# Loading one pair of heads through a second DMA queue and shifting matmuls in an attention + GeGLU kernel

## The chip, the cores and the metric

The kernel runs on one core of a Trainium2 chip. The metric is the device time of one execution in microseconds (us), as the median of several runs. Most executions of one kernel agree within 0.3%. Ratios are the mean time of one kernel's runs over the mean time of the other's in the same rounds, so they are not quite the ratio of the medians quoted beside them. The kernels were measured on different chips. Kernels are compared only within the same rounds.

Names used below: PE is TensorE (matmuls), PEld its weight loads, DVE is VectorE, ACT is ScalarE, POOL is GpSimd, SP is SyncE. "The landing" of a load is the time at which all 16 DMA engines have reported their part.

## The reference

Attention over 8 batches and 8 heads with 16 beacon keys ahead of 576 causal keys, then a GeGLU block over all 4608 tokens.

```python
B, H, S, Nb, D = (8, 8, 576, 16, 64)
k_all = np.concatenate([beacon_k, k], axis=2)          # v_all likewise
scores = scale * np.matmul(q, k_all.transpose(0, 1, 3, 2))
scores = np.where(causal, -1000000000.0, scores)       # only over the 576 keys
a = softmax(scores);  attn = np.matmul(a, v_all)
x = attn.transpose(0, 2, 1, 3).reshape(B * S, H * D)   # 4608 x 512
out = (gelu(x @ w_gate) * (x @ w_val)) @ w_out         # d_ff = 1536
```

## The kernel before

Everything is computed in bf16 with fp32 accumulation. Batch 0 is the start: nothing is on the chip yet, so q and k come in pairs of heads ("pair 0" is heads 0-1, and so on). GpSimd's queue loads them with a cast from fp32 to bf16, TensorE transposes them, and the evictions of those transposes make the operands of the scores.

```python
    load_qk6(0, 0, 2)                # k, then q of heads 0-1, on GpSimd's queue
    load_qk6(0, 2, 4, (1,))          # k of heads 2-3
    # ... GpSimd builds the identity `eye` here
    load_qk6(0, 2, 4, (0,))          # q of heads 2-3
    load_qk6(0, 4, 6)
    load_qk6(0, 6, H)
    # ... then v, the weights, batch 1
```

```python
    warm(66)                         # 66 small matmuls while the loads are under way
    # ... casts of the beacons and the mask, on VectorE
    transpose_both(0, 0)             # pair 0: 12 + 13 transposes, two evictions
    c((0, 0))                        # scores of pair 0, column chunk 0, then ScalarE's exponential
    c((0, 2))
    transpose_both(0, 1)             # pair 1: needs k and q of heads 2-3
    c((0, 1))
    c((1, 0))
    # ... pairs 2 and 3
    c((3, 0))
    c((3, 2))
    av_head(0, 0, 0, psum_t, "t")    # exponentials times v
    av_head(0, 0, 1, psum_o, "o")
    c((2, 3), (3, 3))
    # ... then the first gate/value matmuls of the GeGLU block
```

In batches 1 to 7 the scores and values of batch b are interleaved with the out matmuls of batch b-1; `o(n)` emits the next n of 48. Scores go into three PSUM buffers, and each buffer is free again when ScalarE has taken its exponential.

```python
            o(4)
            scores(b, (0, 0)); scores(b, (0, 2)); scores(b, (0, 1))   # one call per line in the file
            o(5)
            # ...
            o(4)
            scores(b, (0, 3), (1, 3)); scores(b, (1, 0)); scores(b, (1, 2))
            # ...
            o(6)
            av_head(b, 0, 0, psum_t, "t")
            o(1)
            scores(b, (1, 1)); scores(b, (2, 0)); scores(b, (2, 2))
            # ...
            av_head(b, 0, 1, psum_t, "t")
            o(6)
            scores(b, (2, 1)); scores(b, (2, 3), (3, 3)); scores(b, (3, 0))
```

The softmax here doesn't subtract the row's maximum and nothing guards it: scores larger than these inputs give would overflow.

Of the kernel before, what the change touches and what calls it, by code (L numbers as in the profile page):

```python
# [7 lines left out]
P = 128  # L8
B, H, S, NB, D = 8, 8, 576, 16, 64
SK = S + NB  # L10
N_TOK = B * S
D_MODEL = 512
# [28 lines left out]
FP32 = mybir.dt.float32  # L41
# [8 lines left out]
def kernel(  # L50
# [12 lines left out]
    nc = tc.nc  # L63
    keep = tc.keep_in_program_order
# [8 lines left out]
    opool = ctx.enter_context(tc.tile_pool(name="opool", bufs=2))  # L73
# [17 lines left out]
    NRING = 2  # L91
    q_ring, k_ring, v_ring = [], [], []
# [11 lines left out]
    qkT_by_tile = qkT_sb.rearrange("p (w j m c) -> p w j m c", w=2, j=5, m=NPAIR)  # L104
    nc.vector.memset(qkT[:, :, 1, SK:640], 0.0)
    nc.vector.memset(qkT[:, :, 0, 0:NB], 0.0)

    for r in range(NRING):
        nc.vector.memset(q_ring[r][0:32, 0, :, :], 0.0)
        nc.vector.memset(q_ring[r][64:P, 4, :, :], 0.0)  # L110
        nc.vector.memset(k_ring[r][64:P, 4, :, :], 0.0)

    neg = const.tile([P, 256], BF16, name="neg", tag="neg")

    def dma(out_ap, in_ap):
        keep(nc.gpsimd.dma_start(out=out_ap, in_=in_ap))  # L116

    qk6 = {}

    def qk6_of(b):  # L120
        if b not in qk6:
            qk6[b] = (
                hpool.tile([P, 2, H, 6 * D], BF16, name="qk6", tag="hT_sb"),
                kpool.tile([NB, H, D], BF16, name="kb", tag="kb"),
            )
        return qk6[b]

    def load_qk6(b, h0, h1, ws=(1, 0)):
        for w in ws:
            src = (q, k)[w]  # L130
            dma(
                qk6_of(b)[0][0:96, w, h0:h1, :],
                src[b, h0:h1, :, :].rearrange("h (p r) d -> p h (r d)", r=6),
            )
# [18 lines left out]
    def load_qk(b):  # L153
        for load in qk_loads(b):
            load()
# [51 lines left out]
    def transpose_half(b, m, w, by_act=False):  # L207
        pool, tag = ((psum_o, "o"), (psum_t, "t"))[w]
        t_ps = pool.tile([P, 1024], BF16, name="t_ps", tag=tag)
        for _ in range(8 if by_act else 0):  # L210
            tr(t_ps[0:D, 640:768], idle[:, 0:D])
        tr_part(b, m, w, t_ps)
        out_ap = qkT[:, m, w, NB:SK].rearrange("p (t r) -> p t r", r=6)
        in_ap = t_ps[:, 0:S].rearrange("p (r t) -> p t r", r=6)
        if by_act:
            act(out_ap, in_ap, ACT.Copy)
        else:
            keep(nc.vector.tensor_copy(out_ap, in_ap))  # L218
        return t_ps

    def beacon_part(m, t_ps):
        keep(nc.vector.tensor_copy(qkT[:, m, 1, 0:NB], t_ps[:, S:SK]))  # L222

    def transpose_both(b, m):
        k_ps = transpose_half(b, m, 1)
        transpose_half(b, m, 0, by_act=m == 0)
        beacon_part(m, k_ps)
# [86 lines left out]
    def attend(b, m, hi, x_ps):  # L314
        expT, v_sb = exp_ring[:, m, :, :], v_ring[b % NRING]
        for j in range(5):
            for t in range(j + 1):
                e0 = EXP_OFF[t] + (j - t) * P
                mm(
                    x_ps[:, j * DV : (j + 1) * DV],  # L320
                    expT[0 : KROWS[t], hi, e0 : e0 + P],
                    v_sb[0 : KROWS[t], t, 2 * m + hi, 0:DV],
                    t == 0,
                    t == j,
                    skip_group_check=True,
                )
# [26 lines left out]
    def av_head(b, m, hi, pool, tag):  # L353
        x = pool.tile([P, 1, 512], FP32, name="x_ps", tag=tag)
        attend(b, m, hi, x[:, 0, :])
        normalize(b, m, x, hi, hi + 1)
# [39 lines left out]
    def gv_mms(ci, fi, *kks, split=False, last=False):  # L396
        if (ci, fi) not in gv_of:
            if split:
                gv_of[ci, fi] = (
                    psum_t.tile([P, CH], FP32, name="g_ps", tag="t"),  # L400
                    psum_s.tile([P, 2, CH], FP32, name="v_ps", tag="s")[:, 0, :],
                )
            else:
                gv_ps = psum_s.tile([P, 2, CH], FP32, name="gv_ps", tag="s")
                gv_of[ci, fi] = (gv_ps[:, 0, :], gv_ps[:, 1, :])
        n0 = ci * CH

        def part(w):
            for kk in kks:
                mm(  # L410
                    gv_of[ci, fi][w],
                    (wg_sb, wv_sb)[w][:, kk, fi * P : (fi + 1) * P],
                    xT_sb[:, kk, n0 : n0 + CH],
                    kk == 0,
                    last and kk == kks[-1],
                    skip_group_check=True,
                )

        part(0)
        if not split:  # L420
            part(1)
        if not last:
            return
        ge_sb = fpool.tile([P, CH], BF16, name="ge_sb", tag="ge_sb")
        act(ge_sb, gv_of[ci, fi][0], ACT.Gelu)
        if split:
            part(1)
        if ci not in h_of:
            h_of[ci] = hpool.tile([P, F_TILES, CH], BF16, name="hT_sb", tag="hT_sb")
        keep(  # L430
            nc.vector.tensor_tensor(  # L431
                out=h_of[ci][:, fi, :], in0=gv_of.pop((ci, fi))[1], in1=ge_sb, op=ALU.mult
            )
        )
# [30 lines left out]
    def out_mms(ci, u0, u1):  # L465
        for u in range(u0, u1):
# [11 lines left out]
    kb_sb = opool.tile([NB, H, D], FP32, name="kb_sb", tag="o_sb")  # L478
    keep(nc.sync.dma_start(out=kb_sb, in_=beacon_k[0].rearrange("h t d -> t h d")))
    vb_sb = opool.tile([NB, H, D], FP32, name="vb_sb", tag="o_sb")  # L480
    keep(nc.sync.dma_start(out=vb_sb, in_=beacon_v[0].rearrange("h t d -> t h d")))
    load_qk6(0, 0, 2)
    load_qk6(0, 2, 4, (1,))
    keep(
        nc.gpsimd.affine_select(  # L485
            out=eye,
            in_=eye,
# [5 lines left out]
        )  # L493
    )
    load_qk6(0, 2, 4, (0,))
    load_qk6(0, 4, 6)
    load_qk6(0, 6, H)
    for load in key_loads(v, beacon_v, v_ring[0][:, :, :, 0:D], 0)[1:]:
        load()
# [12 lines left out]
    def ahead(n):  # L512
        for load in loads[:n]:
            load()
        del loads[:n]

    ahead(5)

    def c(*parts):
        scores(0, *parts)  # L520

    keep(nc.scalar.preload_act_table_set(SET_EXP))
    warm(66)
    keep(nc.vector.tensor_copy(qk6[0][1], kb_sb))
    keep(nc.vector.tensor_copy(v_ring[0][0:NB, 0, :, 0:D], vb_sb))
    keep(nc.vector.tensor_tensor_scan(neg, eye, idle, -1.0, ALU.add, ALU.add))
    keep(nc.vector.tensor_scalar_mul(neg, neg, -MASKED))
    transpose_both(0, 0)
    c((0, 0))
    c((0, 2))  # L530
    transpose_both(0, 1)
    c((0, 1))
    c((1, 0))
    c((1, 2))
    transpose_both(0, 2)
# [4 lines left out]
    c((2, 2))  # L540
    c((2, 1))
    c((3, 0))
    c((3, 2))
    av_head(0, 0, 0, psum_t, "t")
    av_head(0, 0, 1, psum_o, "o")
    c((2, 3), (3, 3))
    av(0, 1)
    c((3, 1))
# [13 lines left out]
    for kk in (1, 2, 3):  # L562
        for fi in (0, 1):
            gv_mms(0, fi, kk, last=kk == 3)
    for b in range(B):
        u = [0]

        def o(n):
            out_mms(b - 1, u[0], u[0] + n)
            u[0] += n  # L570

        if b:
            keep(nc.scalar.preload_act_table_set(SET_EXP))
            o(4)
            scores(b, (0, 0))
            scores(b, (0, 2))
            scores(b, (0, 1))
            o(5)
            if b == 1:
                transpose_pe(1, 3)  # L580
            ahead(2)
            o(4)
            scores(b, (0, 3), (1, 3))
            scores(b, (1, 0))
            scores(b, (1, 2))
            ahead(2)
            o(6)
            av_head(b, 0, 0, psum_t, "t")
            o(1)
            scores(b, (1, 1))  # L590
            scores(b, (2, 0))
            scores(b, (2, 2))
            ahead(2)
            av_head(b, 0, 1, psum_t, "t")
            turn_dma(b, 0)
            o(6)
            scores(b, (2, 1))
            scores(b, (2, 3), (3, 3))
            scores(b, (3, 0))
            av_head(b, 1, 0, psum_o, "o")  # L600
            o(5)
            av_head(b, 1, 1, psum_o, "o")
            turn_dma(b, 1)
            scores(b, (3, 1))
            scores(b, (3, 2))
            av(b, 2)
            turn_dma(b, 2)
            o(6)
            av(b, 3)
            turn_dma(b, 3)  # L610
            o(11)
            keep(nc.scalar.preload_act_table_set(SET_GELU))  # L612
            for kk in range(K_CHUNKS):
                for fi in range(2):
                    gv_mms(b, fi, kk, last=kk == 3)
        for fi in range(F_TILES):
            if fi >= 2:
                gate_val(b, fi, fi == F_TILES - 1 and b < B - 1)
            if b == 0 and fi in (6, 7, 9):
                transpose_pe(1, min(fi - 6, 2), by_act=True)  # L620
            if fi == 0:
                if b and b + 1 < B:
                    hold(b, 3)
                    load_v(b + 1)
                if b and b + 2 < B:
                    load_qk(b + 2)
                if 2 <= b + 1 < B:
                    transpose_dma(b + 1)
                store(nc.sync)
# [40 lines left out]
```

## Time and profile before

| | before |
|---|---|
| time, median of 3 runs | 367.49 us (367.24 to 367.71) |
| span of the profiled run | 366.2 us |
| PE busy | 355.5 us, 97% |
| first gate/value matmul of the GeGLU block | 22.45 us |
| distance between first scores of neighbouring batches | 39.16 us |

The page of the profile gives busy time per engine first, and then the span in 40 slices, where a digit is the busy share (or the granted TensorE clock) in tenths.

```profile
PE 355.5 (97%) x3127; PEld 183.6 (50%) x3170; DVE 154.8 (42%) x305; ACT 188.8 (52%) x243; POOL 161.7 (44%) x288
...
PE   6899999999999999999999999999999999999996
...
PEclk9999999999999999999999999999999999999999
```

PE is busy nearly everywhere, except in the first slices. So only the start has time to win, besides small stops in the loop. In the start, the chain that ended last (start in us, length in us, what) goes through one load:

```profile
3.83 5.19 DMA qk<-in_q_dram
9.03 0.04 issue
9.07 0.47 PE t_ps L181 x12
9.53 0.02 issue
9.56 0.76 DVE qkT L218
10.31 0.08 DVE qkT L222
10.40 0.05 issue
10.45 0.76 PE s_ps L173 x12
```

The load is q of heads 2-3. It was issued at 3.83 and landed at 9.03, and everything of pair 1 follows it. ScalarE's exponentials of this stage (start, length, group, count, idle time before it and what ended that):

```profile
10.03 9.59 ACT L176 ACTIVATE expT<-s_ps 128x992 bf16<-128x992 f32 x11 [0.68 <-PE s_ps L173]
```

ScalarE runs eleven exponentials without a gap once the scores come, so from 10 to 20 us it sets the pace.

### The profile page before, as it was taken

To read this page: it belongs to the slowest core of one execution; us is meant where nothing else is said; L and a number is where in the kernel's file an instruction comes from. 1 tells how busy PE (TensorE), PEld (TensorE's weight loads), DVE (VectorE), ACT (ScalarE), POOL (GpSimd) and SP (SyncE) were. 2 spreads that over 40 slices of the span, in tenths; PEclk is the share of its full clock that TensorE was granted. 3 is DMA by queue.
4 is the path that set the end of the run, shared out by engine and by line. 5 is a ranking of instruction groups with operands and counts; after the bars stand their busy time and mean duration, and the time that the engine had idled before them with its cause. 6 is when DMAs were issued, how large, how long until landed. Compare 5 with 4: busy or idle time off the path is not lost.

```text
span 366.2 us, 7625 instructions
## 1 busy us (share of the span) xinstructions
PE 355.5 (97%) x3127; PEld 183.6 (50%) x3170; DVE 154.8 (42%) x305; ACT 188.8 (52%) x243; POOL 161.7 (44%) x288
## 2 busy tenths in 40 slices
PE   6899999999999999999999999999999999999996
PEld 6664446444654456444644464445544564444443
DVE  6544545333454335343533354434444353333332
ACT  3973488237933594339723892369334953321210
POOL 8934387565537552845476454656230530000000
PEclk9999999999999999999999999999999999999999
DMA  7999999899069965999299927992795033000103
GB/s 102 172 203 204 197 124 91 135 197 163 20 124 141 213 52 65 163 209 77 56 144 211 122 38 117 170 198 29 100 155 125 11 66 116 0 0 30 57 31 114
DMA packets 160419, 41.57 MB, mean 114 GB/s; under 512 B 146944, under 2 KB 155904, under 8 KB 160384
## 3 DMA queue, kind: packets, MB, share of 16 engines
q0 software_dynamic: 104848, 19.11, 68.9%
q1 hardware_dynamic: 55536, 21.96, 29.7%
q8 instruction: 25, 0.41, 0.5%
q14 instruction: 10, 0.08, 0.1%
HBM read 38.27 MB, written 9.44 MB: 130 GB/s over the span
## 4 chain that ended last, share of the span: by engine, by line
PE 94%; DVE 2%; DMA 1%; issue 1%; POOL 1%; POOLq 0%
PE gv_ps L173 47%; PE o_ps L173 25%; PE x_ps L173 9%; PE s_ps L173 8%; PE v_ps L173 2%; PE g_ps L173 2%; DMA qk<-in_q_dram 1%; PE t_ps L181 1%; DVE qkT L218 1%; POOL qk L116 0%; PE y_ps L181 0%; DVE qkT L200 0%; DVE qkT L204 0%; POOL eye L485 0%; DVE o_sb L450 0%
## 5 line engine op out<-in xcount | busy, mean ns | idle before, releaser
L176 ACT ACTIVATE ge_sb<-gv_ps 128x512 bf16<-128x512 f32 x101 | 59.4, 597 | 142.6 <-PE gv_ps L173 141.5
L431 DVE TENSOR_TENSOR hT_sb<-gv_ps,ge_sb 128x512 bf16<-128x512 f32 x101 | 69.1, 691 | 115.4 <-ACT ge_sb L176 115.4
L173 PE MATMUL gv_ps<-xT_sb,wg_sb 128*128 128x512 bf16 x402 | 111.4, 379 | 0.5
L173 PE MATMUL gv_ps<-xT_sb,wv_sb 128*128 128x512 bf16 x388 | 107.9, 379 | 0.4
L176 ACT ACTIVATE expT<-s_ps 128x992 bf16<-128x992 f32 (+3 forms) x112 | 100.5, 973 | 8.7 <-PE s_ps L173 8.5
L173 PE MATMUL o_ps<-wo_sb,hT_sb 128*128 128x512 bf16 (+2 forms) x420 | 100.6, 373 | 2.1 <-issue 1.1
L303 POOL TENSOR_SCALAR_AFFINE_SELECT expT<-expT 128x256 bf16<-128x256 bf16 (+1 forms) x140 | 52.6, 392 | 53.6 <-ACT expT L176 50.5
L173 PEld LDWEIGHTS <-wv_sb 128*128 128x128 bf16 x432 | 42.2, 98 | 50.6
L173 PEld LDWEIGHTS <-wg_sb 128*128 128x128 bf16 x432 | 42.0, 98 | 50.0
L173 PEld LDWEIGHTS <-hT_sb 128*128 128x128 bf16 x444 | 39.3, 98 | 43.1 <-DVE y_sb L339 3.1
L173 PEld LDWEIGHTS <-expT 128*128 128x128 bf16 (+1 forms) x960 | 33.6, 97 | 9.7 <-DVE y_sb L339 3.1
L450 DVE COPY o_sb<-o_ps 128x512 f32<-128x512 f32 (+2 forms) x37 | 24.9, 672 | 30.3 <-PE o_ps L173 30.2
L173 PE MATMUL x_ps<-v_sb,expT 128*128 128x65 bf16 (+1 forms) x960 | 37.3, 193 | 0.0
L173 PE MATMUL s_ps<-qkT 64*128 64x80 bf16 (+5 forms) x528 | 34.1, 250 | 2.4 <-DVE qkT L222 1.3
L116 POOL DMA_DIRECT2D v_sb<-in_v_dram x40 | 33.7, 860 | 5.9 <-DMA wv_sb<-in_moe_w_val_dram 1.7
L116 POOL DMA_DIRECT2D k_sb<-in_k_dram x30 | 25.2, 846 | 15.9 <-DMA q_sb<-in_q_dram 9.8
L116 POOL DMA_DIRECT2D q_sb<-in_q_dram x30 | 25.4, 876 | 10.3 <-DMA v_sb<-in_v_dram 6.8
L339 DVE TENSOR_TENSOR y_sb<-x_ps,r_sb 128x320 bf16<-128x320 f32 (+1 forms) x47 | 28.8, 612 | 1.6
L337 DVE RECIPROCAL r_sb<-x_ps 128x5 f32<-128x5 f32 (+1 forms) x47 | 9.6, 204 | 45.5 <-PE x_ps L173 45.5
L173 PEld LDWEIGHTS <-qkT 64*128 64x128 bf16 x528 | 17.1, 95 | 18.8 <-issue 12.4
L382 POOL COPY hold_sb<-xT_sb 128x2 bf16<-128x2 bf16 x6 | 1.1, 187 | 31.3 <-DMA xT_sb<-y_sb 31.3
L612 ACT ACT_TABLE_LOAD x7 | 9.0, 1283 | 0.1
(54 smaller groups left out, 116.6 us busy)
## 6 DMA issues: line engine op xcount, KB each, us to landing
out_dram<-o_sb SPq DMA_DIRECT2D x35, 256.0 KB, 7.0
v_sb<-in_v_dram POOLq DMA_DIRECT2D x24, 128.0 KB, 9.0
q_sb<-in_q_dram POOLq DMA_DIRECT2D x18, 128.0 KB, 11.6
k_sb<-in_k_dram POOLq DMA_DIRECT2D x18, 128.0 KB, 5.8
wo_sb<-in_moe_w_out_dram POOLq DMA_DIRECT2D x3, 512.0 KB, 14.4
wg_sb<-in_moe_w_gate_dram POOLq DMA_DIRECT2D x2, 512.0 KB, 11.5
wv_sb<-in_moe_w_val_dram POOLq DMA_DIRECT2D x2, 512.0 KB, 13.2
v_sb<-in_v_dram POOLq DMA_DIRECT2D x8, 112.0 KB, 5.6
```

What stands on the lines that cost most here:

```text
L116: keep(nc.gpsimd.dma_start(out=out_ap, in_=in_ap))
L173: keep(nc.tensor.matmul(out_ap, lhsT, rhs, start=start, stop=stop, **kw))
L176: keep(nc.scalar.activation(out_ap, in_ap, func, **kw))
L181: keep(nc.tensor.transpose(out_ap, in_ap, ident[0:n, 0:n]))
L218: keep(nc.vector.tensor_copy(out_ap, in_ap))
L303: nc.gpsimd.affine_select(out=d, in_=d, pattern=[[0, 2], [1, n]], compare_op=ALU.is_ge, fill=0.0, base=0, channel_multiplier=-1,)
L337: keep(nc.vector.reciprocal(r, x[:, :, :, D:DV]))
L339: nc.vector.tensor_tensor(out=y_of[i][:, :, h0:h1, :].rearrange("p j b d -> p b j d"), in0=x[:, :, :, 0:D], in1=r.to_broadcast([P, h1 - h0 ...
L382: keep(nc.gpsimd.tensor_copy(hold_sb, x[:, 0 : S : S - 1]))
L431: nc.vector.tensor_tensor(out=h_of[ci][:, fi, :], in0=gv_of.pop((ci, fi))[1], in1=ge_sb, op=ALU.mult)
L450: keep(nc.vector.tensor_copy(o_sb[:, ti, c0:c1], o_ps))
L612: keep(nc.scalar.preload_act_table_set(SET_GELU))
```

## The change

Its intent: to move some of the first loads off GpSimd's queue, and to start the values of heads 0-1 one score chunk sooner. k and q of heads 4-5 go through SyncE's queue. They arrive as fp32, because only GpSimd's queue casts (the Trainium skill, "DMA: Bandwidth & Descriptors", SWDGE vs HWDGE vs iDMA, lists casting as possible only there), and VectorE casts them. Six zero fills leave VectorE's first microseconds, and five loads of batch 2 are called behind them. Four counts of out matmuls per batch shift by one or two.

```diff
-    for r in range(NRING):
-        nc.vector.memset(q_ring[r][0:32, 0, :, :], 0.0)
-        ...                                   # three fills for each of two rings; now later
@@ loads of batch 0
     load_qk6(0, 2, 4, (1,))
+    keep(nc.vector.tensor_copy(qk6[0][1], kb_sb))                          # moved up
+    keep(nc.vector.tensor_copy(v_ring[0][0:NB, 0, :, 0:D], vb_sb))         # moved up
     ...
     load_qk6(0, 2, 4, (0,))
-    load_qk6(0, 4, 6)
+    raw = [opool.tile([P, 4, D_MODEL], FP32, name="raw", tag="o_sb")[0:96, 0:2, 0 : 6 * D] for _ in range(2)]
+    for w in (1, 0):
+        keep(nc.sync.dma_start(out=raw[w], in_=(q, k)[w][0, 4:6, :, :].rearrange("h (p r) d -> p h (r d)", r=6)))
     load_qk6(0, 6, H)
     ...
-    ahead(5)                              # five loads of batch 2; moved behind the zero fills
@@ scores of batch 0
     c((0, 2))
+    c((0, 1))
     transpose_both(0, 1)
-    c((0, 1))
+    for w in (1, 0):
+        keep(nc.vector.tensor_copy(qk6[0][0][0:96, w, 4:6, :], raw[w]))
     ...
     c((3, 0))
-    c((3, 2))
     av_head(0, 0, 0, psum_t, "t")
     av_head(0, 0, 1, psum_o, "o")
+    c((3, 2))
@@ batches 1 to 7
-            o(4)      # before scores (0,0)
+            o(3)
-            o(4)      # before scores (0,3),(1,3)
+            o(5)
-            o(6)      # before av_head 0
+            o(5)
-            o(6)      # before scores (2,1)
+            o(7)
```

More of the change, by code (lines that the diff above doesn't have):

```diff
@@ L106 @@
     nc.vector.memset(qkT[:, :, 0, 0:NB], 0.0)
-    for r in range(NRING):
-        nc.vector.memset(q_ring[r][0:32, 0, :, :], 0.0)
-        nc.vector.memset(q_ring[r][64:P, 4, :, :], 0.0)
-        nc.vector.memset(k_ring[r][64:P, 4, :, :], 0.0)
     neg = const.tile([P, 256], BF16, name="neg", tag="neg")
@@ L495 @@
     load_qk6(0, 2, 4, (0,))
-    load_qk6(0, 4, 6)
+    raw = [opool.tile([P, 4, D_MODEL], FP32, name="raw", tag="o_sb")[0:96, 0:2, 0 : 6 * D] for _ in range(2)]
+    for w in (1, 0):
+        keep(
+            nc.sync.dma_start(
+                out=raw[w], in_=(q, k)[w][0, 4:6, :, :].rearrange("h (p r) d -> p h (r d)", r=6)
+            )
+        )
     load_qk6(0, 6, H)
@@ L523 @@
     warm(66)
-    keep(nc.vector.tensor_copy(qk6[0][1], kb_sb))
-    keep(nc.vector.tensor_copy(v_ring[0][0:NB, 0, :, 0:D], vb_sb))
     keep(nc.vector.tensor_tensor_scan(neg, eye, idle, -1.0, ALU.add, ALU.add))
@@ L564 @@
             gv_mms(0, fi, kk, last=kk == 3)
+    for r in range(NRING):
+        keep(nc.vector.memset(q_ring[r][0:32, 0, :, :], 0.0))
+        keep(nc.vector.memset(q_ring[r][64:P, 4, :, :], 0.0))
+        keep(nc.vector.memset(k_ring[r][64:P, 4, :, :], 0.0))
+    ahead(5)
     for b in range(B):
```

## The prediction

> **What bounds the kernel.** The page gives PE 355.5 us busy of a span of 366.2 (97%). In the view of waits, PE waits only 1.0 us after 55 us (six "issue" gaps of 0.16, probably missing records). What is not PE work lies at the start: in the window 0 to 22.5 us PE is busy 18.1. There the chain of waits goes through the load q(heads 2-3), issued at 3.83, landed at 9.03, then transpose, VectorE eviction (0.76), scores. From 10.03 to 19.62 ScalarE runs eleven exponentials without a gap and limits that stage; the last starts at 20.19.
>
> **What the change removes, adds, moves.**
> 1. Six memsets of 0.27 us leave VectorE's first 4 us and go behind the first gate/value matmuls, where VectorE idles. The beacon casts come 0.5 us sooner. The first eviction waits for loads (4.80, 5.68): no gain by itself.
> 2. Two loads (0.63 us of issue each) leave GpSimd's queue for SyncE's, in fp32. They reuse the beacons' buffers, so they issue only after the second beacon cast, about 4.0 and 4.5 us (estimate), first packets 1.0 later, as for the first beacon load. They then share the 16 DMA engines with k and q of heads 2-3, which were ahead of them in one queue before. The Trainium skill ("DMA: Bandwidth & Descriptors", Queues, rings and completion order) says that each engine round-robins between rows with work packet by packet; this trace agrees (from 80.5 to 83 us about 82 packets of each queue per half us). Some 180 packets of 768 B per us moved between 5 and 9 us, and 260 near 29, so there is room, but I expect q(2-3) at about 9.7 (9.3 to 10.3).
> 3. Two casts of 96x768 fp32 on VectorE, about 0.8 us each (estimate from 0.62 for the 16x512 cast), before the evictions of pair 2. They delay scores (2,0) by some 0.4 us, inside ScalarE's backlog.
> 4. Scores (0,1) before the transposes of pair 1 fill a gap on ScalarE, but exponential (1,0) still starts about 1.9 us after q(2-3) lands. So the stage shifts with that landing, +0.7.
> 5. av_head(0,0) before scores (3,2): the gap of 0.57 before the last exponential goes, about -0.4.
> Start in sum: +0.3 us (-0.6 to +1.0).
> 6. Batches 1 to 7: scores (0,0) and (1,1) start one out matmul (0.216) sooner. At 96.28 PE stands 0.17 us before scores (3,0), whose PSUM buffer waits for exponential (2,2) (ends 96.43), back to back since (1,1). That stall recurs in batches 2 to 7 (partly in 1). It should go: about -1.0 us.
>
> **Sum.** 367.49 + 0.3 - 1.0 = 366.8 us, range 365.6 to 368.0. Faster by over 2%: 0.01; within 2%: 0.98; slower by over 2%: 0.01. PE work is unchanged.
>
> **What would show each step.** q(2-3) landing later than 9.03 (2); raw loads landed by about 8.5, casts of about 0.8 (3); exponential (1,0) starting 1.9 us behind that landing (4); no ScalarE gap before the last exponential (5); no 0.17 us PE gap before scores (3,0), and the distance between the first scores of neighbouring batches (39.16 us before) about 0.17 shorter (6).
>
> **What would make it wrong.** The second queue could add throughput without slowing the first: the start gains up to 0.6. Equal sharing could push q(2-3) past 10.5: the start loses over 1 us. Earlier scores could wait for PSUM buffers and bring new stalls, undoing step 6.

## The result and the profile after

The changed kernel took 369.35 us (368.69 to 369.43, 6 runs) against 367.59 (367.24 to 368.21, 6 runs) for the kernel before. The ratio is 1.0045, with a 95% interval of 1.0032 to 1.0058. It is slower by about 1.8 us, still within 2%, but above the predicted range of 365.6 to 368.0.

The same lines of the page as before:

```profile
PE 355.5 (97%) x3127; PEld 185.7 (51%) x3170; DVE 156.5 (43%) x307; ACT 189.1 (51%) x243; POOL 160.1 (44%) x286
...
PE   6799999999999999999999999999999999999996
...
PEclk9699999999999999999999999999999999999999
```

The new sight is the 6 in the second slice of the granted clock. The records of the clock put it at exactly half from 11.00 to 17.82 us. PE's summed busy time is the same by coincidence: up to the first gate/value matmul it rose from 18.05 to 19.81 us, as matmuls in the slow stretch took longer, and from there on it fell from 337.43 to 335.73.

The chain through the start:

```profile
3.85 6.74 DMA qk<-in_q_dram
10.59 0.04 issue
10.64 0.47 PE t_ps L176 x12
11.10 0.02 issue
11.12 0.76 DVE qkT L213
11.88 0.08 DVE qkT L217
11.97 0.05 issue
12.01 1.31 PE s_ps L168 x9
```

q of heads 2-3 was issued at the same time as before and landed at 10.59 instead of 9.03. The nine score matmuls behind it took 1.31 us at half clock, where twelve took 0.76. SyncE's loads, from the list of DMA issues (KB each, median us from issue to landing), needed longer than GpSimd's in the kernel before (4.9 and 5.3):

```profile
raw<-in_k_dram SPq DMA_DIRECT2D x1, 288.0 KB, 6.2
raw<-in_q_dram SPq DMA_DIRECT2D x1, 288.0 KB, 7.2
```

They were issued at 3.16 and 3.67 us, so they were under way while k and q of heads 2-3 were. ScalarE's exponentials of this stage, which ran without a gap from 10.03 on before, now wait three times:

```profile
12.82 1.86 ACT L171 ACTIVATE expT<-s_ps 128x1024 bf16<-128x1024 f32 x2 [2.79 <-PE s_ps L168]
15.51 2.67 ACT L171 ACTIVATE expT<-s_ps 128x832 bf16<-128x832 f32 x3 [0.83 <-PE s_ps L168]
18.47 5.38 ACT L171 ACTIVATE expT<-s_ps 128x928 bf16<-128x928 f32 x6 [0.29 <-PE s_ps L168]
```

The first wait is for the late landing; the other two fall into the stretch of half clock or just behind it. The first scores of batches 2 and 3 in the timelines show the other side; first the kernel before, then the kernel after:

```profile
87.51 0.73 PE L173 MATMUL s_ps<-qkT 64*128 64x512 bf16 x10
...
126.67 0.81 PE L173 MATMUL s_ps<-qkT 64*128 64x512 bf16 x14
```

```profile
89.83 0.77 PE L168 MATMUL s_ps<-qkT 64*128 64x512 bf16 x11
...
128.71 0.77 PE L168 MATMUL s_ps<-qkT 64*128 64x512 bf16 x12
```

The distance fell from 39.16 to 38.88 us. So the kernel after loses 2.76 us before the first gate/value matmul (25.21 against 22.45), and then wins back 0.28 us in nearly every batch.

### The profile page after: what moved, and what is told of

Read it like the earlier page. It is cut to its first block, busy times and chain, and to the rows that moved or that the text cites. A ratio compares the mean times of both kernels' runs of the same rounds, so it can differ in the third digit from the quotient of the medians.

```text
span 367.4 us, 7630 instructions
## 1 busy us (share of the span) xinstructions
PE 355.5 (97%) x3127; PEld 185.7 (51%) x3170; DVE 156.5 (43%) x307; ACT 189.1 (51%) x243; POOL 160.1 (44%) x286
## 4 chain that ended last, share of the span: by engine, by line
PE 94%; DMA 2%; issue 1%; ACT 1%; POOL 1%; DVE 0%; POOLq 0%
PE gv_ps L168 47%; PE o_ps L168 25%; PE x_ps L168 8%; PE s_ps L168 8%; DMA qk<-in_q_dram 2%; PE t_ps L176 2%; PE v_ps L168 2%; PE g_ps L168 2%; ACT expT L171 1%; POOL qk L111 0%; PE y_ps L176 0%; DVE qkT L213 0%; POOL eye L482 0%; DVE o_sb L445 0%; DVE r_sb L332 0%
## 5 line engine op out<-in xcount | busy, mean ns | idle before, releaser
L176 PE MATMUL t_ps<-eye,qk 96*64 96x96 bf16 x192 | 7.4, 226 | 2.2 <-DMA qk<-in_k_dram 1.1
```

Source lines behind the costliest of these rows:

```text
L176: keep(nc.tensor.transpose(out_ap, in_ap, ident[0:n, 0:n]))
```

## The experiments

Thirteen kernels ran, all with correct results. "Before" in a result is the kernel before. My theory after seeing the result: SyncE's loads share the DMA engines with the loads that TensorE waits for next (the late landing), the late landing leaves TensorE too idle to keep its clock (the half clock), and the loop's gain is real. Rivals: the new order of scores and values costs the time, or the casts on VectorE do, or the gain of the loop comes from elsewhere.

### 1. Only the loop's counts (e1_loop_only)

```diff
  kernel before
-            o(4) ... o(4) ... o(6) ... o(6)
+            o(3) ... o(5) ... o(5) ... o(7)
```

> The kernel before with only the four moved out-matmul counts of batches 1 to 7. In the profile of after, the distance between first scores of neighbouring batches fell from 39.16 to 38.88 us, and from 40.06 to 39.83 for the first. If that comes from the moved counts alone, six such steps and the first give 6 x 0.28 + 0.23 = 1.9 us: time about 365.7 (before 367.6), period 38.88, start unchanged (first gate/value matmul at 22.45). Rival: the gain of the loop comes from something else in the change (or is given back at the end): 367.3 to 367.8.

Measured: 366.46 us against 367.48, ratio 0.9967 (0.9953 to 0.9981). The five distances from batch 2 on were 38.88, but the first one stayed at 40.06, so its 0.23 us in the profile of after comes from something else, which I did not find. (The record narrows it: the first distance is 39.83 to 39.85 in every kernel that has both the new counts and a load less on GpSimd's queue, and 40.05 to 40.06 in all others.) The loop's counts are worth 5 x 0.28 = 1.4 us in the trace and 1.0 to 1.2 us of the time. Less than expected, but they are worth it alone.

### 2. All loads on GpSimd's queue, the rest of the change kept (e2_pool_loads)

```diff
  kernel after
-    raw = [...]; two loads on nc.sync; two casts on nc.vector
+    load_qk6(0, 4, 6)
```

> The kernel after with k and q of heads 4-5 loaded by GpSimd's queue with its cast, as before, and without the two VectorE casts; all else of the change stays. Theory (the second queue is the loss): q of heads 2-3 lands at 9.0 again instead of 10.59, the granted clock stays 1.0, the first gate/value matmul comes at 22.4 or sooner, and the loop's 1.9 us remain: time 365.2 to 365.8. Rival (the new order of scores, values or zero fills at the start costs the time): the first gate/value matmul stays near 24 to 25 us and the time near 368 to 369.

Measured: 366.41 us against 367.48, ratio 0.9967 (0.9953 to 0.9980). q of heads 2-3 landed at 8.56 us and the first gate/value matmul came at 22.25. The time is that of the run with the loop's counts alone, so the new order of scores, values, zero fills and later loads is worth nothing measurable, and it costs nothing measurable; the two intervals leave room for some 0.5 us either way. The 365.2 to 365.8 that I expected was too low because the loop gave less. The rival of the new order falls. What SyncE's loads and their casts cost is the difference of +1.76 and -1.07 us against the kernel before, 2.8 us.

One part did not fit: the clock did not stay at 1.0 in all runs. In the profile it was half for 3.41 us from 11.40 on.

### 3. Fillers to keep the clock (e4_fill)

```diff
  kernel after, transpose_both of pair 1
+            fill(psum_t, "t", 20)      # 20 matmuls of 64 columns on zeros
         k_ps = transpose_half(b, m, 1)
+            fill(psum_o, "o", 20)
         transpose_half(b, m, 0, by_act=m == 0)
```

> The kernel after with 20 matmuls of 64 columns on zeros ahead of each of the two transpose groups of pair 1, where TensorE only waits for k and q of heads 2-3 (1.1 us each). Nothing lands sooner. Theory (part of the loss is the clock that the late landing halves from 11.0 to 17.8 us): the clock stays 1.0, q still lands near 10.6, first gate/value matmul near 24.0 instead of 25.2, time about 368.1 (after 369.35). Rival (the landing alone makes the whole loss, the clock costs nothing as ScalarE sets the pace): 369.2 to 369.5 with the clock at 1.0.

Measured: 368.64 us (367.66 to 369.26) against 367.48, ratio 1.0022 (1.0006 to 1.0038). The clock stayed at 1.0 in the profile, q landed at 10.54 and the first gate/value matmul came at 23.64, as the theory has it. But then TensorE stood still:

```profile
25.39 0.38 PE L168 MATMUL gv_ps<-xT_sb,wg_sb 128*128 128x512 bf16 x1 [0.90 <-issue]
```

"issue" means that no wait which the profile shows explains the 0.90 us. So the time fell by only half of what the first mark had promised. Inconclusive by itself; experiment 8 says more of the stop.

### 4. SyncE's loads held back (e5_raw_late)

```diff
  kernel after; the two loads now stand behind transpose_both(0, 0)
+    late = const.tile([P, 16], BF16, name="late", tag="late")
+    keep(nc.sync.dma_start(out=late[0:1, :], in_=qkT[0:1, 0, 1, NB : NB + 16]))   # waits for an eviction
     raw = [...]; two loads on nc.sync
```

> The kernel after with the two fp32 loads held back on SyncE's queue by a 32-byte copy that waits for the first VectorE eviction (about 6.0 us), so that they are issued at about 6.6 and 7.0 instead of 3.16 and 3.67. Theory (the two queues share the DMA engines, and what SyncE's loads move before q of heads 2-3 is done delays it): q of heads 2-3 lands at 9.3 to 9.8, clock 1.0, time 366.0 to 367.2. Rival (the delay does not depend on when the loads are issued): q lands near 10.6, time near 369.

Measured: 370.92 us against 367.48, ratio 1.0088 (1.0074 to 1.0103): a miss in the time, though the part about sharing held. q of heads 2-3 landed at 7.97 us, which is sooner than in any kernel so far, as SyncE's queue moved no load beside it then. But SyncE's two loads, issued at 7.07 and 7.69, now shared them with v and landed at 13.70 and 15.00. The waits of PE from 3 to 30 us show who paid (us in total, times, longest):

```profile
PE t_ps L176 <- DVE qk L535: 3.7, 2, 3.2
```

PE waits for the casts of pair 2. So here as in the kernel after, the overlap of the queues delayed the load that was wanted next. The clock, which I had expected at 1.0, was half from 12.41 to 19.24, so the time has that loss in it too. I had expected that late loads would be in time for pair 2, and had not worked out how slow they get beside v.

### 5. Only SyncE's loads and casts (e3_raw_only)

```diff
  kernel before
-    load_qk6(0, 4, 6)
+    the beacon casts, then raw = [...] and two loads on nc.sync
     c((0, 1))
+    two casts of raw on nc.vector
```

> The kernel before with only the two fp32 loads on SyncE's queue and their casts (the beacon casts stand ahead of them in the program, behind the six zero fills on VectorE as before, so the loads are issued at about 4.0 and 4.6 us). Loop, order of scores, values and fills as before. Theory (the second queue is what costs): q of heads 2-3 lands at 9.8 to 10.6, first gate/value matmul at 23.8 to 25.3, periods 40.06 and 39.16 as before, time 369.0 to 370.5. Rival (the loads cost only together with the new order): within 0.4 us of before.

Measured: 370.78 us (368.49 to 372.32) against 367.59, ratio 1.0082 (1.0055 to 1.0108). q landed at 10.56, the first gate/value matmul came at 25.42, and the distances were 40.05 and 39.16. The loads alone make the loss. The rival that they cost only together with the new order falls. The runs spread widely, and they go by the mean granted clock: 368.49 at 1.0, 369.81 at 0.995, 370.70 to 372.32 at 0.990 to 0.991.

### 6. Half the dose (e6_k_only)

```diff
  kernel after
+    raw = one tile; k of heads 4-5 on nc.sync, cast on nc.vector
+    load_qk6(0, 4, 6, (0,))      # q of heads 4-5 on GpSimd's queue again
```

> The kernel after with half the dose: only k of heads 4-5 on SyncE's queue in fp32, q of heads 4-5 on GpSimd's queue behind q of heads 2-3. Theory (SyncE's packets take turns with GpSimd's, so the delay goes with the bytes that SyncE moves meanwhile): q of heads 2-3 lands about half way between 8.6 to 9.0 (without) and 10.6 (with both), 9.4 to 9.9; time about 367.3 to 368.3. Rival (any traffic on the second queue costs the whole delay): 10.4 to 10.6 and 369.

Measured: 368.00 us (366.58 to 368.69) against 367.59, ratio 1.0008 (0.9990 to 1.0027). q of heads 2-3 landed at 9.35 us, between 8.56 (none on SyncE's queue) and 10.59 (both). The delay goes with the amount moved, as far as one point between two can tell, and the rival that any traffic costs the whole falls. The times go by the clock here too: 366.58 and 366.71 at 1.0 and 0.995, and 367.88 to 368.69 in the four runs at 0.985 to 0.990.

### 7. The traffic without its use (e9_traffic_only)

```diff
  the kernel of experiment 2
     load_qk6(0, 4, 6)
+    raw = [...]; the two loads on nc.sync, read by nobody
```

> The run with all loads on GpSimd's queue (366.4 us) plus the two fp32 loads on SyncE's queue as in after, which nobody reads: the traffic without the VectorE casts and without moving pair 2. Theory (the traffic alone delays q of heads 2-3): it lands at 10.2 to 10.7, the clock drops as in after, time 368.8 to 370.5. Rival (the casts or the way of pair 2 through them make the loss): q may land late, but the time stays below 367.2.

Measured: 369.13 us (367.99 to 369.86) against 367.56, ratio 1.0038 (1.0022 to 1.0053), where the same kernel without the traffic had 0.9967. q landed at 10.07. No cast and no detour of pair 2 is there, and the loss is nearly whole, so it is the traffic. (There is more of it in all than in the kernel after, as GpSimd's queue loads pair 2 too. And the clock was half for only 3.42 us in the profile, not as in after.) The rival of the casts falls; they took 0.55 to 0.74 us each in the kernel after.

How the two queues shared the engines can be counted in the trace's records of DMA packets, those with data that started from 5 to 9 us:

| kernel | GpSimd's queue | SyncE's queue | sum | q of heads 2-3 landed |
|---|---|---|---|---|
| before | 690 | 0 | 690 | 9.03 |
| experiment 2 | 682 | 0 | 682 | 8.56 |
| experiment 6 (k only) | 525 | 189 | 714 | 9.35 |
| after | 396 | 341 | 737 | 10.59 |
| experiment 7 | 382 | 360 | 742 | 10.07 |

Packets can be compared by number, as one of either queue carries 384 values (768 bytes in bf16, 1536 in fp32). In these rows the second queue adds 7 to 9%. But the sums vary from profile to profile: over all seven that issue both loads on SyncE's queue from 3.2 to 4.2 us they are 629 to 787, against 661 to 690 in three with GpSimd's queue alone (before, experiments 1 and 2); the control of experiment 9, the same kernel as after, has 641. So most of what SyncE's queue moves is taken from GpSimd's, which fell to 311 to 417. That the engines could not move more is not shown: in the profile of e8 (experiment 10) GpSimd's queue alone moved 921 packets of 768 bytes in the same 4 us. Why is open. The sharing is what the Trainium skill says in "DMA: Bandwidth & Descriptors", Issuing engines are not separate DMA queues: DMAs started by different engines end up on the same 16 DMA engines and interleave.

### 8. More and other fillers (e4b_fill56, e4c_wide_fill)

```diff
  as experiment 3
-            fill(psum_o, "o", 20)
+            fill(psum_o, "o", 36)     # e4b;  e4c: 8 and 10 fillers of 256 columns
```

> As the run with 20 and 20 fillers, with 20 and 36. There the clock stayed 1.0 and the first gate/value matmul came at 23.64, but then TensorE stood 0.9 us for nothing that the profile shows. If the clock is worth what that first mark says (25.21 to 23.64), a run without such a stop takes 367.6 to 368.0; runs with it 368.5 to 368.9. Rival (the clock is worth only the 0.7 us of the medians): 368.6 also without the stop.

> The kernel after with 8 and 10 fillers of 256 columns (36 added TensorE instructions with their weight loads, against 80 and 112 in the two filler runs that showed a stop of about 1 us further on). Theory (the clock is worth about 1.5 us of the start, and the stop comes with the number of added instructions): clock 1.0, no stop, first gate/value matmul at 23.6 to 23.9, time 367.6 to 368.1. Rival (filling itself costs, the clock is worth 0.7 us or less): 368.5 to 369.2.

Measured: e4b 369.12 us against 367.59 (ratio 1.0045, 1.0031 to 1.0058) and e4c 369.52 against 367.56 (1.0051, 1.0032 to 1.0069). Both kept the clock within 0.999 to 1.0 in all runs but one, and neither was faster than the kernel after. The profile of e4b again has a stop near 24 us that nothing explains:

```profile
24.58 0.43 PE L168 MATMUL x_ps<-v_sb,expT 128*128 128x65 bf16 x9 [0.99 <-issue]
```

The profile of e4c has none there, but in it q of heads 0-1 landed 1.1 us later than in the others (6.67) and a matmul at 304.93 waited 0.91 us for a DMA transpose. So adding matmuls disturbed more than it told. My guess that the stop comes with the number of added instructions was not confirmed by the times.

The traces have a lead that no experiment tested. They show 16 KB packets on a queue named "instruction". In both profiles with a stop, it ends as TensorE starts the 962nd of its recorded matmuls and weight loads, 2.30 and 2.28 us after the third of these packets started (23.09 and 22.31). In the thirteen other profiles TensorE came to that place 5.2 to 10.6 us after that packet. So the stop looks like a wait for the next part of the program: the fillers of experiment 3 and e4b added 80 and 112 TensorE instructions (a matmul counts with its weight load), those of e4c only 36. If all their runs had it, those two kernels would take 367.7 and 368.1 us without it (an estimate, 368.64 - 0.90 and 369.12 - 0.99).

### 9. The same number of matmuls, moved (after_again, e10_even_fill)

To keep the clock without adding an instruction, half of the 66 warm-up matmuls moved. The control ran on the same chip.

```diff
  kernel after
-    warm(66)                          # 64 columns each
+    warm(33)                          # 128 columns each
+            fill(psum_t, "t", 14)     # 128 columns each, ahead of the transposes of k
+            fill(psum_o, "o", 19)     # ahead of those of q
```

> The kernel after unchanged, as the control for the next run on the same chip: 369.0 to 369.6, granted clock 0.989 to 0.995.

> The kernel after with 33 of its 66 warm-up matmuls moved to where TensorE waits for k and q of heads 2-3 (14 and 19 of 128 columns; the 33 that stay have 128 columns instead of 64, so the warm-up is as long and the number of TensorE instructions is the same). Theory (the halved clock is worth 1.2 to 1.5 us between the landing of q and the first gate/value matmul, and the earlier filler runs lost that again in stops that came with their added instructions): clock 1.0, no stop near 24 us, first gate/value matmul 13.1 to 13.6 us behind the landing of q (14.6 in after), time 1.0 to 1.6 us below the control. Rival (the clock is worth little in the whole kernel; the late landing is the loss): within 0.5 us of the control.

Measured: the control 368.17 us (367.59 to 369.41) and the moved fillers 368.04 (367.71 to 368.32), both against 367.45; ratios 1.0017 (1.0002 to 1.0032) and 1.0012 (1.0000 to 1.0024). By the medians the rival wins, but the runs of the control show two groups:

| mean granted clock | kernel after, first time | control | moved fillers |
|---|---|---|---|
| 0.999 to 1.0 | none | none | 367.71, 367.89, 368.04, 368.04, 368.32 |
| 0.995 (half for 3.4 us in the profiles that have it) | 368.69 | 367.59, 367.69, 368.10, 368.25 | none |
| 0.989 to 0.991 (half for 6.8 us) | 369.32, 369.32, 369.38, 369.39, 369.43 | 369.31, 369.41 | none |

On one chip, the mean is 368.0 at full clock, 367.9 at 0.995 and 369.4 at 0.989. So the runs with the long drop of the clock took 1.4 us more, and those with the short one nothing that is seen here. (The one run at 0.995 in the first measurement was only 0.7 us below the others.) The same grouping gives 1.5, 1.6 and 1.0 us in experiments 5, 6 and 7, as means of the runs at 0.985 to 0.991 less those at 0.995 or more (in experiment 5 the single run at 0.995). Groups of runs can differ in more than the clock, so the profiles have to agree. First the kernel after from 7.60 us on, then the moved fillers; each line is a stretch of the span with busy time by engine, then the granted clock:

```profile
7.60:11.00 3.40, 1.21 (x37) 0.88 (x33) 0.76 (x1) 2.43 (x3) 2.49 (x4) 1.00 1.37 196
11.00:17.80 6.80, 5.87 (x96) 4.16 (x94) 3.71 (x8) 4.15 (x5) 6.02 (x9) 0.50 1.93 175
```

```profile
7.60:11.00 3.40, 3.29 (x76) 2.98 (x70) 0.76 (x1) 2.60 (x3) 2.61 (x4) 1.00 1.47 209
11.00:17.80 6.80, 5.02 (x131) 3.54 (x125) 4.92 (x10) 5.13 (x7) 5.58 (x9) 1.00 1.93 175
```

PE (the first busy time) is busy 1.21 of 3.40 us in the kernel after while it waits for k and q, and then gets half the clock: 96 matmuls take 5.87 us, where 131 take 5.02 at full clock. From the landing of q to the first gate/value matmul it is 25.21 - 10.59 = 14.62 us in the kernel after, 25.29 - 10.50 = 14.79 in the control's profile, and 24.02 - 10.46 = 13.56 with the moved fillers. The landing is nearly the same in the three, so it does not make this difference. Other profiles fall in line: 14.86 in experiment 5 (long drop), 13.69, 13.69 and 13.70 in experiments 2, 6 and 7 (short drop), 13.10 and 13.54 with the fillers of experiment 3 and e4c (full clock); e4b's 14.63 contains its stop of 0.99. (e5, e7 and e8 load in another order and are left out.) And the waits of ScalarE behind the landing went, of which the kernel after has 0.83 and 0.29 us; here a gap of 0.42 is left at the end:

```profile
12.67 8.66 ACT L171 ACTIVATE expT<-s_ps 128x1024 bf16<-128x1024 f32 x10 [2.47 <-PE s_ps L168]
```

### 10. Two attempts at a faster version (e7_first_pair, e8_k0_sync)

Both start from experiment 2 and use SyncE's queue at 0.8 us, when it is alone.

```diff
  e7: k and q of heads 0-1 in fp32 on nc.sync, casts on nc.vector; warm(54); GpSimd's queue starts with k of heads 2-3
  e8: only k of heads 0-1 so; GpSimd's queue starts with q of heads 0-1
```

> An attempt to use SyncE's queue where nothing else is under way: k and q of heads 0-1 in fp32 on SyncE's queue from 0.8 us on, with VectorE's casts (0.61 each in the trace of after), all other loads on GpSimd's queue, which starts with k of heads 2-3; zero fills late and the loop as in after; 54 warm-up matmuls instead of 66. If early sharing is cheap: k and q of heads 0-1 usable at about 4.1 and 4.9 (4.6 and 5.6 without), q of heads 2-3 at 6.5 to 7.3 instead of 8.6, first gate/value matmul near 21, time 365.0 to 365.8. If GpSimd's queue, running from 2.9 us, delays SyncE's loads as much as the reverse in after: k and q no sooner than before, time 366 or more.

> An attempt at a faster version on the run with all loads on GpSimd's queue: only k of heads 0-1 goes in fp32 on SyncE's queue at 0.8 us, where it is alone for the first microsecond; GpSimd's queue starts with q of heads 0-1 and is one load ahead from then on. If the two split the engines only until about 4 us: k usable at about 4.8 (4.6 before), q at about 4.8 (5.6), q of heads 2-3 at 7.6 to 8.2 (8.56), first gate/value matmul at 21.4 to 21.9, time 365.5 to 366.1. If sharing costs here too: q of heads 2-3 no sooner than 8.5 and 366.4 or more.

Measured: e7 370.74 us against 367.59 (ratio 1.0086, 1.0072 to 1.0101). k of heads 0-1 landed at 4.13, but q only at 7.10, while GpSimd's loads of pair 1 were under way too, from 3 us on. The clock spoils this comparison: in the profile its records begin only at 17.28, and up to there score matmuls of 512 columns started 189 to 200 ns apart, against 107 to 113 at full clock in the other profiles. It was half from the start, which the mean of 1.0 given for this run does not show, as time before the first record counts as full. e8: 366.33 us (365.58 to 369.01) against 367.56 (0.9973, 0.9950 to 0.9996). Five of its six runs were at 0.999 to 1.0 of the clock and took 365.58 to 366.64; one at 0.985 took 369.01. In the profile, which is of the slow one of the six, q of heads 2-3 landed at 7.93. It is not told apart from experiments 1 and 2 (366.46 and 366.41), which are the best versions found: about 1.1 us faster than the kernel before.

## Why the prediction was wrong

The time was predicted as 367.49 + 0.3 - 1.0 = 366.8 us, and 369.35 was measured. Point by point:

- **Bound by PE, only the start and small stops can move: right.** The change moved 0.5% in all.
- **Step 1, fills and beacon casts gain nothing by themselves: right** (experiment 2 equals experiment 1). The fills ran at 31 to 33 us, not in the gap that VectorE had at 24.72 to 27.05 in the kernel before.
- **Step 2, "q(2-3) at about 9.7 (9.3 to 10.3)": the mechanism was right, the size was not.** It landed at 10.59 and 10.50. The failing term is "there is room": I took 260 packets per us near 29 us, from another stage, as what both queues could reach between 5 and 9 us. There the two moved 737 packets in 4 us, 184 per us, where one queue alone moved 690. SyncE's 341 packets came with 294 fewer of GpSimd's. The loads were also issued sooner (3.16 and 3.67) than the 4.0 and 4.5 that I had estimated, because the fills no longer stood ahead of the beacon casts, which step 1 itself says.
- **Step 3, casts "about 0.8 us each": too high.** They took 0.55 and 0.74 us.
- **Step 4, "exponential (1,0) still starts about 1.9 us after q(2-3) lands. So the stage shifts with that landing": incomplete.** It started at 12.82, 2.23 us behind. This is the second failing step: the sum has no term for TensorE's clock. While it waited for k and q, TensorE was busy for only 1.22 of 3.41 us, and then its granted clock was half from 11.0 to 17.8 us. The runs that had this, five of the first six, took 1.4 us more where full clock and half clock were compared on one chip (experiment 9). The Trainium skill describes such a gate ("TensorE: Matmul & The Clock Gate", Part 1: The HAM clock gate), with half rate after an idle window of about 3.4 us; here the 3.41 us ahead of the drop were not all idle. I had read the full clock of the kernel before as a fact and not as something that a longer wait can lose.
- **Step 5, no gap before the last exponential: right in kind.** 0.04 us of ScalarE's idle time was left there, instead of 0.57. By experiment 2 it is worth nothing measurable in the time.
- **Step 6, "about -1.0 us" in the loop: right.** Alone it gave 1.0 to 1.2 us. In the trace each of five distances is 0.28 us shorter and not 0.17: the stop of 0.17 before scores (3,0) went, and so did one of 0.11 between two out matmuls, where the next out tile had waited for its PSUM buffer. I had not counted that one.

The sum with measured terms, for the first measurement: loop about -1.1, new order about 0, late landing about +1.5, half clock +1.4, which makes +1.8 (measured +1.76). The sum closes by construction, as the share of the landing is what is left of 2.8 us without the clock's 1.4; the runs at full clock say the same, 368.0 with fillers against 366.4 without SyncE's loads, 1.6 us.

That the clock is the cause of the 1.4 us rests on the two groups of the control, on the moved fillers, of which no run had a drop, and on the two waits of ScalarE that went with it. The first three filler runs did not show it in their times. In the control the loss against before was only 0.17% (0.7 us), as four of its six runs had the short drop; so what the change costs varies from run to run of the same kernel, and which drop a run gets was not controlled.

## What to carry to other kernels

In this start, loads moved to a second queue got little bandwidth of their own: they took turns with what was ahead of them. So ask which load is wanted next and what the moved one takes from it, in the rate of that very stage. When a change makes TensorE wait longer, look at the granted clock of the next microseconds as well as at the wait, compare runs of equal clock, and check from when on the clock was recorded. Fillers that keep the clock are not free: two sets of them came with a stop of about 1 us further on. Where a change bundles parts, run the parts alone: here one was worth -1.1 us and another +2.8.

## What the Trainium skill lacked or had wrong

- "TensorE: Matmul & The Clock Gate" (Part 1, and its closing table) speaks of idle gaps of about 3 us or more, and in Part 1 also of micro-idles between groups of matmuls, without a figure for how much idle time is enough. Here the clock halved although no single wait was longer than 1.1 us: in the 3.41 us ahead of the drop TensorE was still busy 1.22 us in the kernel after and 2.27 us in experiment 2.
- The same page (Part 4: PE-mode transpose) remarks that transposes do not count as busy in the same way. The runs agree and give numbers. Busy time without the transposes in the window of 3.41 us ahead: 0.00 to 0.76 us in the eight windows that were followed by half clock from full clock (0.76 in experiment 2), 0.86 us or more in those that kept it (1.27 at the same place in the kernel before, with 2.10 in all). The drops lasted 3.41, 6.83 or 10.24 us. What ends one is not settled: behind a drop, windows with 2.12 to 2.14 us (at half rate) were followed by full clock and those with 1.71 or less were not, but in e7, at half clock from the start, a window with 2.49 us of warm-up matmuls was not either. These come from the thirteen profiles that record the clock of the start (not e7 and experiment 1) and are an observation, not a rule.
- "DMA: Bandwidth & Descriptors" (Queues, rings and completion order) says that engines take turns between queues by packets and gives no figure for what a second queue adds in sum. Here it added little: 629 to 787 packets in 4 us in seven profiles with it, 661 to 690 in three without.
- The stops of 0.90 and 0.99 us of TensorE near 24 us in two of the filler runs: no page gives a duration for such a stop. If they are a wait for instructions, as the lead in experiment 8 suggests, they belong to "Runtime: NRT & Kernel Launch". None of the other profiles has one there.
